# Attention and gated FFN in one kernel: a lead-in with 64x64 state products, one multiplication moved to GpSimd, and later scores for some pairs

## The chip, the cores and the metric

The kernel runs on one core of one Trainium2 chip. The metric is the device time of one execution in microseconds, the median of several runs. TensorE does the matrix products (PE in the profile), VectorE is DVE, ScalarE is ACT, GpSimd is POOL and SyncE is SP. DMAs are asked for by an instruction on SP, ACT or POOL and move data on 16 DMA engines.

## The reference, cut to what matters

Two layers run one after the other. The first is linear attention with decay, for 4 batches, 8 heads, 768 tokens and head size 64, in blocks of 64 tokens with a state of 64x64 for each head:

```python
for b in range(nb):
    intra = einsum('bhic,bhjc->bhij', qb, kb) * Dmask      # scores, masked
    intra = einsum('bhij,bhjd->bhid', intra, vb)           # values
    inter = einsum('bhid,bhde->bhie', qb * lam_pow, kv_state)
    out[:, :, sl] = intra + inter
    kv_state = lam_block * kv_state + einsum('bhsd,bhse->bhde', kb_dec, vb)
```

The second is a feed-forward layer on the 3072x512 result: `h = x @ w_in` (512x2048), `g = h * cos(h)`, and the output `g @ w_out` (2048x512).

## The kernel before, in words

**Tiles.** The tokens are cut into 24 blocks of 128. Two blocks, one from each of two batches, make a pair. The feed-forward layer takes the blocks in tiles of 4, 2, 2, 2, 2, 2, 2, 4 and 4. For each tile it makes 16 hidden blocks (`hidden`, L729 to L734: four matmuls each, with 128 columns of `w_in` as weights and the tile's tokens moving), turns each into `g` by a cosine on ACT (L738) and a product on DVE (L744), and multiplies by `w_out` (`project`, L774 to L779).

**The lead-in.** The first four blocks are two spans of 256 tokens, built in `add_span` (L579 to L687). A span is loaded as one DMA for q and one for k (SP, 512 KB each) and one for v (POOL). q and k are multiplied by powers of the decay (`prep`, L592), in two halves of four heads (hp 0 and 1); they are turned on PE (L601) and copied out by ACT (L604). Then come the scores (L612), their mask on DVE (L617, four for each span), the state product of k and v (`update`, L620 to L626), its copy into a block-diagonal tile (`update_out`, L629), the values (L638), the part that the state carries over (L644), and the copy of the result into `xT` (L652). `QK`, `OUTS`, `VALUES_OUT` and `STATE_OUT` (L32 to L35) say which engine does which of these for span 0 and span 1. In the kernel before DVE does all of span 0's `prep` and span 1's q, and POOL does span 1's k.

**The first tile's hidden blocks.** Blocks f = 0 to 4 of tile 0 are made in two halves of 256 columns, `a` for the tokens of span 0 and `b` for those of span 1. Blocks 3a and 4a are ordered behind span 1's last product (L849). `w_in` comes in six pieces of 2, 2, 1, 3, 4 and 4 blocks (`W_IN`, L38), asked for on POOL with a conversion to bf16: piece 1 holds f = 0 and 1, piece 2 f = 2 and 3, piece 3 f = 4, piece 4 f = 5 to 7, piece 5 f = 8 to 11, piece 6 f = 12 to 15. Then come three pieces of `w_out`. Before, the third piece's request waits for span 1's k on POOL:

```python
            if x:
                w_t["in", 2].issue.deps.append(kt[hp])
```

**What sets the order.** A planner (`Planner`, L57 to L141) lays out all tasks ahead of time with costs, due times, PSUM banks and buffers; each engine then runs its tasks in the order of the planned starts. `SETUP` holds the time at which each engine is taken to be free, and each task's second argument its cost. So a changed cost changes the order of instructions and nothing else. From pair 3 on, q and k are turned by DMA (`transposes_dma`, L364); the planner takes their result as ready 1.2 us after the DMA's planned end (`T[pr, i].lat`, L372). Pairs 3 to 6 (`ALONE`) have scores and state products as a group of their own; later pairs have theirs inside the stretch of the pair before (`add_scores`, L394, and `add_stretch`, L458).

**Fill.** Until the first hidden block of 512 columns (f = 5), `keep_awake` (L861 to L871) puts matmuls without use into PE's planned gaps, in fp32 from a zeroed tile `blank`, or one of 512 columns in bf16 from the identity where the gap is 0.25 to 0.6 us.

Of the kernel before, what the change touches and what calls it, by code (L numbers as in the profile page):

```python
# [10 lines left out]
F32 = mybir.dt.float32  # L11
BF16 = mybir.dt.bfloat16
# [12 lines left out]
ATT = 0.95  # L25
LOAD_US = 1.22
ALONE = [3, 4, 5, 6]

APART = [3, 4, 5, 11]


QK = [{"q": ("DVE", "DVE"), "k": ("DVE", "DVE")}, {"q": ("DVE", "DVE"), "k": ("POOL", "POOL")}]  # L32
OUTS = [{"qT": ("ACT", "ACT"), "kT": ("ACT", "ACT")}, {"qT": ("ACT", "ACT"), "kT": ("ACT", "ACT")}]
VALUES_OUT = [("ACT", "ACT"), ("DVE", "ACT")]
STATE_OUT = [("ACT", "ACT"), ("ACT", "ACT")]  # L35
ORDER = "q0 k0 q1 k1 v0 v1 i0 i1 i2 i3 i4 i5 o0 o1 o2 q4 q5 k4 k5 o3"

W_IN = [2, 2, 1, 3, 4, 4]  # L38
# [18 lines left out]
class Planner:  # L57
# [1 line left out]

    LAT = {"PE": 0.2, "ACT": 0.06, "DVE": 0.08, "POOL": 0.1, "SP": 0.0, "DMA": 0.0, "SETUP": 0.0}  # L60

    SETUP = {"POOL": 3.7, "DVE": 4.4, "ACT": 6.0, "SP": 0.85, "DMA": 1.95}

    def __init__(self, bufs):
        self.tasks, self.bufs = [], bufs
# [79 lines left out]
def kernel(  # L145
# [10 lines left out]
    nc = tc.nc  # L156
    B, H, S, D = q.shape
    P = 128
# [19 lines left out]
    consts = ctx.enter_context(tc.tile_pool(name="consts", bufs=1))  # L178
# [16 lines left out]
    ident = consts.tile([P, P], BF16)  # L195
# [15 lines left out]
                                base=0, pattern=[[1, D]], channel_multiplier=-1)  # L211
    halfpi = consts.tile([P, 1], F32)
    nc.vector.memset(halfpi, math.pi / 2.0)
    blank = consts.tile([P, 4 * P], F32)
    nc.vector.memset(blank, 0.0)  # L215
    kv_bd = consts.tile([P, 2, NP, P], BF16)
    nc.vector.memset(kv_bd, 0.0)

# [8 lines left out]
    pl = Planner({**BUFS, "q_f": BUFS["ld"], "k_f": BUFS["ld"], "v_f": BUFS["ld"]})  # L227
# [3 lines left out]
    halves = [slice(i * D, (i + 1) * D) for i in range(2)]  # L231
# [60 lines left out]
    w_t, pace = {}, []  # L292
# [15 lines left out]
    T, So, Vo, d_t, Uo, Uo_sp = ({} for _ in range(6))  # L308
# [6 lines left out]
    def prepare(pr):  # L315

        b, c = where(2 * pr)
        early = 2 * pr < TILES[0] + 2
        vec = {"DVE": nc.vector, "POOL": nc.gpsimd}
        us = {"DVE": 0.69, "POOL": 1.05}  # L320
        pa = lambda part: prio_attn(2 * pr, part)

        def new_qk():
            if ("qk", pr) not in live:
                live["qk", pr] = toks.tile([P, 2, H, 2, D], BF16, tag="qk", bufs=BUFS["qk"], name="qk")
            return live["qk", pr]

        def prep_q(_, s, e):
            vec[e].tensor_mul(new_qk()[:, 0, :, s], live.pop(("q_f", 2 * pr + s)),  # L329
                              q_scale[:, c, :].unsqueeze(2).to_broadcast([P, H, D]))  # L330

        def prep_k(_, s):
            (nc.scalar.copy if early else nc.gpsimd.tensor_copy)(new_qk()[:, 1, :, s], live.pop(("k_f", 2 * pr + s)))  # L333

        def prep_v(_, s, e):
            live["v_s", 2 * pr + s] = toks.tile([P, H, D], BF16, tag="v_s", bufs=BUFS["v_s"], name="v_s")
            vec[e].tensor_mul(live["v_s", 2 * pr + s], live.pop(("v_f", 2 * pr + s)),  # L337
                              v_scale[:, c, :].unsqueeze(2).to_broadcast([P, H, D]))

        a, k_ = [], []  # L340
        for s in range(2):
            n = 2 * pr + s
            eq = "DVE" if early and s == 0 else "POOL"
            ev = "DVE" if early and s == 1 else "POOL"
            a.append(pl.add(eq, us[eq], [load_t["q_f", n]] + a, partial(prep_q, s=s, e=eq), pa(-0.9), get=None if s else "qk"))
            k_.append(pl.add("ACT" if early else "POOL", 0.61, [load_t["k_f", n]] + ([] if early else [a[0]]), partial(prep_k, s=s), pa(-0.9)))
            d_t[n] = v_head[n] = pl.add(ev, us[ev], [load_t["v_f", n]], partial(prep_v, s=s, e=ev), pa(-0.85), get="v_s")
            for name, t in (("q_f", a[s]), ("k_f", k_[s]), ("v_f", d_t[n])):
                issue_t[name, n].frees = [t]

        def new_T():
            if ("qkT", pr) not in live:
                live["qkT", pr] = toks.tile([P, 2, H, P], BF16, tag="qkT", bufs=BUFS["qkT"], name="qkT")
            return live["qkT", pr]

        def transposes(t, i):
            live["t", pr, i] = bank(t.bank[0], [P, H, P], BF16, "ps_t")
            for h in range(H):
                nc.tensor.transpose(live["t", pr, i][:, h, :], live["qk", pr][:, i, h], ident)  # L359

        def transposes_out(_, i):
            nc.vector.tensor_copy(new_T()[:, i], live["t", pr, i])

        def transposes_dma(_, i):  # L364
            return nc.sync.dma_start_transpose(out=new_T()[:, i], in_=live["qk", pr][:, i].rearrange("t h s d -> t (h s d)"))

        for i, src in enumerate((a, k_)):
            get = None if i else "qkT"
            if 2 * pr >= DMA_FROM:
                head, T[pr, i] = dma("SP", 1.4, 1.3, partial(transposes_dma, i=i), 2 * pr + i - LAG + 1.5,  # L370
                                     src + ([qkT_head[pr]] if i else []), get=get, ordered=False)
                T[pr, i].lat = 1.2  # L372
                if i and 2 * pr + LAG < NBLK:
                    issue_t["q_f", 2 * pr + LAG].deps.append(head)
            else:
                t = pl.add("PE", MM(P, 8), src + ([T[pr, 0]] if i else []), partial(transposes, i=i), pa(-0.05 + 0.05 * i), banks=1)
                head = T[pr, i] = pl.add("DVE", 0.7, [t], partial(transposes_out, i=i), pa(0.0), get=get)
                t.bank_frees = [[head]]
            if i == 0:
                qkT_head[pr] = head  # L380
        qk_head[pr] = a[0]
# [194 lines left out]
    spans, span_deps = [], []  # L576
    span_v = [consts.tile([P, H, 2, D], BF16, name=f"v_sp{x}") for x in range(SPANS)]

    def add_span(x):  # L579
        pa = lambda part: -1000.0 + 2 * x + part  # L580
        pv = lambda part: -990.0 + 2 * x + part
        cut = [slice(4 * hp, 4 * hp + 4) for hp in range(2)]
        us = {"DVE": 0.69, "POOL": 1.04}
        vec = {"DVE": nc.vector, "POOL": nc.gpsimd}
        L = {name: consts.tile([P, 2, H, D], BF16, name=f"{name}_sp{x}") for name in ("q", "k")}
        L["v"] = span_v[x].rearrange("u h s d -> u s h d")
# [33 lines left out]
        def update(t):  # L620
            L["kv"] = bank(t.bank[0], [P, NP, P], F32, "ps_kv")
            rows = chunks[0][0]
            for p in range(NP):
                for s in range(2):
                    nc.tensor.matmul(L["kv"][:, p, :], lhsT=L["k"][rows, s, 2 * p:2 * p + 2, :], rhs=L["v"][rows, s, 2 * p:2 * p + 2, :],  # L625
                                     start=(p == 0 and s == 0), stop=True, skip_group_check=True)  # L626

        def update_out(_, h, e):
            (nc.scalar.copy if e == "ACT" else nc.vector.tensor_copy)(kv_bd[h, x, :, h], L["kv"][h, :, h])  # L629
# [27 lines left out]
        for hp in range(2):  # L657
# [1 line left out]
            a = pl.add(eq, us[eq], [load_t["q_f", "sp", x]], partial(prep, name="q", hp=hp, e=eq), pa(-0.9 + 0.1 * hp))  # L659
            kt.append(pl.add(ek, us[ek], [load_t["k_f", "sp", x]], partial(prep, name="k", hp=hp, e=ek), pa(-0.9 + 0.1 * hp)))  # L660
            if x:
                w_t["in", 2].issue.deps.append(kt[hp])
            outs = []
            for name, src in (("qT", a), ("kT", kt[hp])):
                e = OUTS[x][name][hp]
                t = pl.add("PE", MM(P, 4), [src, s_first if name == "kT" else None], partial(transposes, name=name, hp=hp), pa(-0.5 + 0.1 * hp), banks=1)
                outs.append(pl.add(e, 0.58 if e == "ACT" else 0.42, [t], partial(transposes_out, name=name, hp=hp, e=e), pa(-0.5 + 0.1 * hp)))
                t.bank_frees = [[outs[-1]]]
            s1 = pl.add("PE", 0.42, outs, partial(scores, hp=hp), pa(0.1 + 0.1 * hp), banks=2)
            if x and hp == 0:  # L670
                s_first = s1
            so[hp] = [pl.add("DVE", 0.69, [s1], partial(scores_out, hp=hp, i=i), pa(0.1 + 0.1 * hp + 0.05 * i)) for i in range(2)]
            s1.bank_frees = [[t] for t in so[hp]]

        u = pl.add("PE", 0.42, v_t + kt + [spans[0].get("carried")], update, pv(0.1), banks=1)
        Uo_sp[x] = [pl.add(e, 0.4 if e == "ACT" else 0.42, [u], partial(update_out, h=h, e=e), pv(0.1))
                    for h, e in zip(halves, STATE_OUT[x])]
        u.bank_frees = [Uo_sp[x]]
        span_deps.extend(v_t + kt)
        v0 = pl.add("PE", 0.35, so[0] + v_t + [spans[0].get("carried")], partial(values, hp=0), pv(0.2), banks=2)  # L680
        v1 = pl.add("PE", 0.35, [v0] + so[1], partial(values, hp=1), pv(0.25))
        second = pl.add("PE", MM(P, 4) + 0.1, [v1] + Uo_sp[x], carried, pv(0.3))
        for c, (t, e) in enumerate(zip((v1, second), VALUES_OUT[x])):
            Vo[2 * x + c] = [pl.add(e, 0.6 if e == "ACT" else 0.69, [t], partial(values_out, c=c, e=e), pv(0.3) if c == 0 else -1200.0)]
# [156 lines left out]
    pr = SPANS  # L841
# [16 lines left out]
    tc.plan = plan  # L858
    idle_ps = bank(idle.bank[0], [P, 4 * P], F32, "ps_idle")

    def keep_awake(us, at):  # L861

        cols = int((us - 0.06) * (1200.0 if at < 7.0 else 2400.0) / 4) // 64 * 64
        if us < 0.6:
            if us > 0.25:
                nc.tensor.matmul(idle_ps, lhsT=ident, rhs=ident.unsqueeze(1).to_broadcast([P, 4, P]), start=True, stop=True)
            return
        while cols > 0:
            n = min(cols, 4 * P)
            nc.tensor.matmul(idle_ps[:, :n], lhsT=blank[:, :P], rhs=blank[:, :n], start=True, stop=True)  # L870
            cols -= n  # L871

    keep_awake(1.2, 1.6)
    lam_ps = bank((idle.bank[0] + 4) % BANKS, [P, H], F32, "ps_lam")
    nc.tensor.matmul(lam_ps, lhsT=ones, rhs=lam_row, start=True, stop=True)
    lnl = consts.tile([P, H], F32)
# [14 lines left out]
    nc.scalar.activation(v_scale, expo, AF.Exp, scale=-1.0)  # L891
    warm = consts.tile([P, 1], F32)
    nc.scalar.activation(warm, halfpi, AF.Sin)
    now = 2.8
    for t in plan:
        if t.eng == "PE" and t.start < lead_end.start + 1e-6:
            keep_awake((t.start - now) * 0.95 if now < 3.0 else t.start - now, now)
            now = t.end
        if t.emit:
            t.ins = t.emit(t)  # L900

# [29 lines left out]
```

## Time and profile before

| What | Value |
|---|---|
| time, median of 3 runs | 202.96 us (202.85 to 203.05) |
| the profiled execution: its own time | 202.54 us |
| the profiled execution: its span, first to last instruction | 200.8 us |
| PE, PEld (weight load), DVE, ACT, POOL busy | 195.9, 116.8, 116.3, 119.4, 64.9 us |
| granted TensorE clock | 0.998 |
| HBM read and written | 27.26 and 6.29 MB |

All positions below are microseconds from the first instruction of the profiled execution. A line of the timeline gives the start, the length from the first start to the last end, the engine and the source line, what is written and read, and how many instructions are merged. Matmuls overlap in their records, so the start of the next group tells more than the end of the one before. A view of a tile gives, for each DMA request that it catches, the time from the request to the landing of the data.

### The profile page before, as it was taken

The numbers are of one execution on the slowest core, as the hardware profiler recorded it, in microseconds if no ns is written. First come the engines' busy times: TensorE is split into PE (matmuls) and PEld (weight loads), VectorE is DVE, ScalarE is ACT, GpSimd is POOL, SyncE is SP. The second block draws the span as 40 slices with busy tenths as digits, with TensorE's granted clock in tenths as the row PEclk, the third lists the DMA queues.
The fourth block names the chain that finished last, engine by engine and source line by source line (L and its number), as shares of the span: only waits on it lengthen the run. The fifth ranks groups of instructions, "written<-read, shape, count | busy, mean of one in ns | idle before, by whom it ended". The sixth has DMA issues, their size and how long they took to land.

```text
span 200.8 us, 5951 instructions
## 1 busy us (share of the span) xinstructions
PE 195.9 (98%) x2473; PEld 116.8 (58%) x2473; DVE 116.3 (58%) x230; ACT 119.4 (59%) x241; POOL 64.9 (32%) x85
## 2 busy tenths in 40 slices
PE   6999999999999999999999999999999999999994
PEld 3477444558757757766658676755445544444452
DVE  3978771269756948758458575835588354444001
ACT  4878771149658768666639666644887564345120
POOL 5893003085235360635555353545500000000000
PEclk9999999999999999999999999999999999999999
DMA  5999999999889997999999899979910010111112
GB/s 163 303 190 204 203 199 216 209 238 225 200 197 225 262 202 177 239 179 253 189 275 245 188 207 194 277 141 261 243 23 3 3 52 0 52 55 52 52 52 104
DMA packets 96620, 33.93 MB, mean 169 GB/s; under 512 B 84690, under 2 KB 93650, under 8 KB 96594
## 3 DMA queue, kind: packets, MB, share of 16 engines
q1 hardware_dynamic: 89088, 28.78, 63.2%
q0 software_dynamic: 7360, 4.72, 16.4%
q8 instruction: 19, 0.31, 0.7%
q10 hardware_dynamic: 146, 0.07, 0.1%
q14 instruction: 7, 0.06, 0.1%
HBM read 27.26 MB, written 6.29 MB: 167 GB/s over the span
## 4 chain that ended last, share of the span: by engine, by line
PE 95%; DMA 2%; ACT 0%; DVE 0%; SPq 0%; issue 0%; ACTq 0%; DVEq 0%
PE ps_h L732 42%; PE ps_f L778 42%; DMA sp_f<-in_k_dram 2%; PE ps_s L407 2%; PE ps_o L502 2%; PE ps_o L470 2%; PE ps_kv L419 1%; PE ps_t L601 1%; PE ps_s L612 1%; PE ps_o L638 1%; PE ps_kv L625 1%; PE ps_x L470 0%; PE ps_idle L870 0%; PE ps_t L359 0%; DVE k_sp L593 0%; PE ps_o L644 0%
## 5 line engine op out<-in xcount | busy, mean ns | idle before, releaser
L744 DVE TENSOR_TENSOR g<-ps_h,cos 128x256 bf16<-128x256 f32 (+1 forms) x149 | 73.1, 501 | 42.0 <-ACT cos L738 41.1
L738 ACT ACTIVATE cos<-ps_h,halfpi 128x256 f32<-128x256 f32 (+1 forms) x149 | 75.9, 536 | 29.3 <-PE ps_h L732 28.2
L778 PE MATMUL ps_f<-w_out_sb,g 128*128 128x512 bf16 (+2 forms) x400 | 91.4, 371 | 0.0
L732 PE MATMUL ps_h<-xT,w_in_sb 128*128 128x256 bf16 (+1 forms) x596 | 91.1, 303 | 0.0
L732 PEld LDWEIGHTS <-w_in_sb 128*128 128x128 bf16 x596 | 57.5, 98 | 30.1 <-DVE xT L510 0.4
L778 PEld LDWEIGHTS <-g 128*128 128x128 bf16 x400 | 37.6, 98 | 37.2
L329 POOL TENSOR_TENSOR qk<-q_f,q_scale 128x512 bf16<-128x512 f32 x19 | 20.0, 1067 | 34.7 <-DMA q_f<-in_q_dram 17.6
L792 ACT COPY o_sb<-ps_f 128x512 f32<-128x512 f32 (+1 forms) x24 | 13.7, 572 | 24.7 <-PE ps_f L778 24.5
L337 POOL TENSOR_TENSOR v_s<-v_f,v_scale 128x512 bf16<-128x512 f32 x19 | 19.6, 1042 | 9.8 <-DMA v_f<-in_v_dram 5.2
L412 DVE TENSOR_TENSOR s_m<-ps_s,mask 128x512 bf16<-128x512 f32 x20 | 13.0, 685 | 4.2 <-PE ps_s L407 3.6
L333 POOL CAST qk<-k_f 128x512 bf16<-128x512 f32 x18 | 11.0, 611 | 10.4 <-DMA k_f<-in_k_dram 10.2
L510 ACT CAST xT<-ps_o 128x512 bf16<-128x512 f32 x11 | 6.0, 588 | 9.0 <-PE ps_o L502 5.6
L425 DVE TENSOR_TENSOR sum<-sum,ps_kv 128x512 f32<-128x512 f32 x15 | 10.2, 682 | 0.6
L430 ACT CAST S<-sum 128x512 bf16<-128x512 f32 x15 | 9.1, 616 | 0.9 <-DVE sum L425 0.8
L253 POOL DMA_DIRECT2D w_out_sb<-in_moe_w_out_dram x4 | 3.0, 784 | 15.8 <-DMA q_f<-in_q_dram 15.8
L792 DVE COPY o_sb<-ps_f 128x384 f32<-128x384 f32 x1 | 0.6, 557 | 11.6 <-DMA out_dram<-o_sb 11.6
L470 PEld LDWEIGHTS <-v_s 64*64 64x64 bf16 x320 | 4.0, 107 | 4.2 <-issue 3.4
L870 PE MATMUL ps_idle<-blank 128*128 128x512 f32 (+2 forms) x8 | 4.7, 707 | 1.7 <-DVE blank L215 1.7
L487 DVE COPY spare<-ps_o 1x1 f32<-1x1 f32 x6 | 0.9, 156 | 8.4 <-PE ps_o L470 8.4
L617 DVE TENSOR_TENSOR s_m_sp<-ps_s,mask_sp 128x512 bf16<-128x512 f32 x8 | 5.1, 684 | 1.2 <-PE ps_s L612 1.2
L470 PE MATMUL ps_o<-s_m,v_s 64*64 64x64 bf16 x256 | 5.2, 196 | 0.0
L502 PE MATMUL ps_o<-qkT,S 64*64 64x64 bf16 x304 | 4.9, 195 | 0.0
(76 smaller groups left out, 90.1 us busy)
## 6 DMA issues: line engine op xcount, KB each, us to landing
q_f<-in_q_dram SPq DMA_DIRECT2D x20, 256.0 KB, 3.9
k_f<-in_k_dram SPq DMA_DIRECT2D x20, 256.0 KB, 4.2
v_f<-in_v_dram SPq DMA_DIRECT2D x20, 256.0 KB, 5.1
out_dram<-o_sb SPq DMA_DIRECT2D x19, 256.0 KB, 2.5
w_out_sb<-in_moe_w_out_dram POOLq DMA_DIRECT2D x4, 512.0 KB, 12.4
sp_f<-in_q_dram SPq DMA_DIRECT2D x2, 512.0 KB, 4.9
sp_f<-in_k_dram SPq DMA_DIRECT2D x2, 512.0 KB, 5.5
w_in_sb<-in_moe_w_in_dram POOLq DMA_DIRECT2D x2, 512.0 KB, 8.9
```

The source lines that it names most:

```text
L329: vec[e].tensor_mul(new_qk()[:, 0, :, s], live.pop(("q_f", 2 * pr + s)), q_scale[:, c, :].unsqueeze(2).to_broadcast([P, H, D]))
L333: (nc.scalar.copy if early else nc.gpsimd.tensor_copy)(new_qk()[:, 1, :, s], live.pop(("k_f", 2 * pr + s)))
L337: vec[e].tensor_mul(live["v_s", 2 * pr + s], live.pop(("v_f", 2 * pr + s)), v_scale[:, c, :].unsqueeze(2).to_broadcast([P, H, D]))
L412: nc.vector.tensor_mul(t, live["s", pr][s], mask.unsqueeze(1).to_broadcast([P, H, D]))
L425: nc.vector.tensor_add(new, live["sum", pr, 0] if half else live["sum", pr - 1, 1], live["kv", pr][half])
L430: nc.scalar.copy(new_S(pr, half), live["sum", pr, half])
L470: yield lambda h=h: nc.tensor.matmul(o[halves[h % 2], h // 2], lhsT=live["v_s", n0 + s][m, h, :], rhs=live["s_m", n0 + s][m, h, :], start= ...
L732: nc.tensor.matmul(t[:, :n], lhsT=w_in_sb[:, kd, f * P:(f + 1) * P], rhs=live["xT", i][:, kd, at], start=(kd == 0), stop=(kd == KD - 1))
L738: nc.scalar.activation(c[:, :n], live["h", i, f, at.start][:, :n], AF.Sin, bias=halfpi)
L744: return nc.vector.tensor_mul(live["g", i][:, f, at], live.pop(("h", i, f, at.start))[:, :n], live.pop(("c", i, f, at.start))[:, :n])
L778: nc.tensor.matmul(live["f", i, j, piece][:, :width], lhsT=live["g", i][:, f, j * P:(j + 1) * P], rhs=w_out_sb[:, f, part], start=(f == 0) ...
L792: (nc.scalar.copy if eng == "ACT" else nc.vector.tensor_copy)(o[:, :width], live["f", i, j, piece][:, :width])
```

## The change

The state products of a span become 16 matmuls of 64x64 instead of 8 of 64x128. Span 1's second q half goes from DVE to POOL, the second half of span 0's state copy and the second of its two copies into `xT` go from ACT to DVE. The request for piece 2 of `w_in` (and so all requests behind it on POOL) goes behind span 1's k, instead of that for piece 3. The transposes of pairs 4 to 9 are planned as ready later. Some planned costs are altered. The tile `blank` and its memset go; the fill reads a constant of one that the program's start sets, in fp32 and in bf16, with other lengths, and a fill is put behind the products with the decay.

```diff
+T_LAT = {4: 3.0, 5: 3.0, 6: 3.0, 7: 2.5, 8: 2.5, 9: 2.5}
-QK = [{"q": ("DVE", "DVE"), "k": ("DVE", "DVE")}, {"q": ("DVE", "DVE"), "k": ("POOL", "POOL")}]
+QK = [{"q": ("DVE", "DVE"), "k": ("DVE", "DVE")}, {"q": ("DVE", "POOL"), "k": ("POOL", "POOL")}]
-VALUES_OUT = [("ACT", "ACT"), ("DVE", "ACT")]
-STATE_OUT = [("ACT", "ACT"), ("ACT", "ACT")]
+VALUES_OUT = [("ACT", "DVE"), ("DVE", "ACT")]
+STATE_OUT = [("ACT", "DVE"), ("ACT", "ACT")]
-    SETUP = {"POOL": 3.7, "DVE": 4.4, "ACT": 6.0, "SP": 0.85, "DMA": 1.95}
+    SETUP = {"POOL": 3.7, "DVE": 4.2, "ACT": 6.1, "SP": 0.85, "DMA": 1.95}
-    blank = consts.tile([P, 4 * P], F32)
-    nc.vector.memset(blank, 0.0)
-                T[pr, i].lat = 1.2
+                T[pr, i].lat = T_LAT.get(pr, 1.2)
-        us = {"DVE": 0.69, "POOL": 1.04}
+        us = {"DVE": 0.62, "POOL": 1.02}
                 for s in range(2):
-                    nc.tensor.matmul(L["kv"][:, p, :], lhsT=L["k"][rows, s, 2 * p:2 * p + 2, :], rhs=L["v"][rows, s, 2 * p:2 * p + 2, :],
-                                     start=(p == 0 and s == 0), stop=True, skip_group_check=True)
+                    for i, h in enumerate(halves):
+                        nc.tensor.matmul(L["kv"][h, p, h], lhsT=L["k"][rows, s, 2 * p + i, :], rhs=L["v"][rows, s, 2 * p + i, :],
+                                         start=(p == 0 and s == 0), stop=True, skip_group_check=True)
             if x:
-                w_t["in", 2].issue.deps.append(kt[hp])
+                w_t["in", 1].issue.deps.append(kt[hp])
-            s1 = pl.add("PE", 0.42, outs, partial(scores, hp=hp), pa(0.1 + 0.1 * hp), banks=2)
+            s1 = pl.add("PE", 0.33, outs, partial(scores, hp=hp), pa(0.1 + 0.1 * hp), banks=2)
-        u = pl.add("PE", 0.42, v_t + kt + [spans[0].get("carried")], update, pv(0.1), banks=1)
+        u = pl.add("PE", 0.28, v_t + kt + [spans[0].get("carried")], update, pv(0.1), banks=1)
...
-    keep_awake(1.2, 1.6)
+    def ones_of(n, dt=BF16):
+        one = nc.const_aps.tensor(1.0, [P, 4 * P], dt)
+        nc.tensor.matmul(idle_ps[:, :n], lhsT=one[:, :P], rhs=one[:, :n], start=True, stop=True)
+
+    def keep_awake(us, slow):
+        if slow:
+            cols = min(int((us - 0.04) * 1200.0) // 64 * 64, 4 * P)
+            if cols > 0:
+                ones_of(cols)
+        elif us > 0.8:
+            ones_of(min(int((us - 0.25) * 600.0) // 64 * 64, 4 * P), F32)
+        elif us > 0.5:
+            ones_of(4 * P)
+
+    ones_of(4 * P, F32)
...
+    ones_of(4 * P, F32)
+    now = None
     for t in plan:
         if t.eng == "PE" and t.start < lead_end.start + 1e-6:
+            slow = t.start < 8.5
+            if now:
+                keep_awake(t.start - now, slow)
+            now = max(t.end, t.start + 0.4) if slow else t.end
```

The planned costs of the masks (0.69 to 0.61) and of the values (0.35 to 0.33) are altered in the same way.

More of the change, by code (lines that the diff above doesn't have):

```diff
@@ L668, in add_span @@
                 t.bank_frees = [[outs[-1]]]
-            s1 = pl.add("PE", 0.42, outs, partial(scores, hp=hp), pa(0.1 + 0.1 * hp), banks=2)
+            s1 = pl.add("PE", 0.33, outs, partial(scores, hp=hp), pa(0.1 + 0.1 * hp), banks=2)
             if x and hp == 0:
                 s_first = s1
-            so[hp] = [pl.add("DVE", 0.69, [s1], partial(scores_out, hp=hp, i=i), pa(0.1 + 0.1 * hp + 0.05 * i)) for i in range(2)]
+            so[hp] = [pl.add("DVE", 0.61, [s1], partial(scores_out, hp=hp, i=i), pa(0.1 + 0.1 * hp + 0.05 * i)) for i in range(2)]
             s1.bank_frees = [[t] for t in so[hp]]
-        u = pl.add("PE", 0.42, v_t + kt + [spans[0].get("carried")], update, pv(0.1), banks=1)
+        u = pl.add("PE", 0.28, v_t + kt + [spans[0].get("carried")], update, pv(0.1), banks=1)
         Uo_sp[x] = [pl.add(e, 0.4 if e == "ACT" else 0.42, [u], partial(update_out, h=h, e=e), pv(0.1))
@@ L679, in add_span @@
         span_deps.extend(v_t + kt)
-        v0 = pl.add("PE", 0.35, so[0] + v_t + [spans[0].get("carried")], partial(values, hp=0), pv(0.2), banks=2)
-        v1 = pl.add("PE", 0.35, [v0] + so[1], partial(values, hp=1), pv(0.25))
+        v0 = pl.add("PE", 0.33, so[0] + v_t + [spans[0].get("carried")], partial(values, hp=0), pv(0.2), banks=2)
+        v1 = pl.add("PE", 0.33, [v0] + so[1], partial(values, hp=1), pv(0.25))
         second = pl.add("PE", MM(P, 4) + 0.1, [v1] + Uo_sp[x], carried, pv(0.3))
@@ L859 @@
     idle_ps = bank(idle.bank[0], [P, 4 * P], F32, "ps_idle")
[L861 to L871, printed above, removed]
-    keep_awake(1.2, 1.6)
+    def ones_of(n, dt=BF16):
[11 more added lines that the diff above has]
+    ones_of(4 * P, F32)
     lam_ps = bank((idle.bank[0] + 4) % BANKS, [P, H], F32, "ps_lam")
@@ L893 @@
     nc.scalar.activation(warm, halfpi, AF.Sin)
-    now = 2.8
+    ones_of(4 * P, F32)
+    now = None
     for t in plan:
         if t.eng == "PE" and t.start < lead_end.start + 1e-6:
-            keep_awake((t.start - now) * 0.95 if now < 3.0 else t.start - now, now)
-            now = t.end
+            slow = t.start < 8.5
+            if now:
+                keep_awake(t.start - now, slow)
+            now = max(t.end, t.start + 0.4) if slow else t.end
         if t.emit:
```

## The prediction, made before the changed kernel ran

> **What bounds the kernel now.** I first read the page's busy times and the list of PE's waits.
>
> ```profile
> PE 195.9 (98%) x2473; PEld 116.8 (58%) x2473; DVE 116.3 (58%) x230; ACT 119.4 (59%) x241; POOL 64.9 (32%) x85
> PE ps_idle L870 <- DVE blank L215: 1.7, 1, 1.7
> PE ps_t L601 <- DVE k_sp L593: 0.3, 1, 0.3
> ```
>
> PE waits twice, both before 7.1 us. The chain of waits agrees: from 7.08 to 197.9 it is PE alone, 95% of the span. Its long pieces run at one rate (64 hidden matmuls of 256 columns in 7.02 us, 0.110 us each; 28 of 512 in 6.04 us, 0.216 us each). So no wait is left to remove after the lead-in. Next I read PE's timeline of the lead-in.
>
> ```profile
> 9.23 0.40 PE L601 MATMUL ps_t<-ident,q_sp 128*128 128x128 bf16 x4
> 9.47 1.08 PE L870 MATMUL ps_idle<-blank 128*128 128x512 f32 x2
> 10.57 0.40 PE L601 MATMUL ps_t<-ident,k_sp 128*128 128x128 bf16 x4
> 10.90 0.62 PE L625 MATMUL ps_kv<-v_sp,k_sp 64*128 64x128 bf16 x8
> 11.45 0.42 PE L638 MATMUL ps_o<-s_m_sp,v_sp 64*64 64x128 bf16 x16
> 11.69 0.39 PE L612 MATMUL ps_s<-qT_sp,kT_sp 64*64 64x128 bf16 x16
> 12.02 0.40 PE L601 MATMUL ps_t<-ident,k_sp 128*128 128x128 bf16 x4
> 12.35 0.42 PE L638 MATMUL ps_o<-s_m_sp,v_sp 64*64 64x128 bf16 x16
> 12.70 0.40 PE L644 MATMUL ps_o<-qT_sp,kv_bd 128*128 128x128 bf16 x4
> 13.03 0.62 PE L625 MATMUL ps_kv<-v_sp,k_sp 64*128 64x128 bf16 x8
> 13.57 0.42 PE L612 MATMUL ps_s<-qT_sp,kT_sp 64*64 64x128 bf16 x16
> 13.82 0.39 PE L638 MATMUL ps_o<-s_m_sp,v_sp 64*64 64x128 bf16 x16
> 14.14 1.48 PE L732 MATMUL ps_h<-xT,w_in_sb 128*128 128x256 bf16 x12
> 15.56 0.42 PE L638 MATMUL ps_o<-s_m_sp,v_sp 64*64 64x128 bf16 x16
> 15.91 0.40 PE L644 MATMUL ps_o<-qT_sp,kv_bd 128*128 128x128 bf16 x4
> ```
>
> The useful stream starts at 10.57, when POOL has scaled the first half of span 1's k: it lands at 9.3 and POOL starts at 9.47 (1.04 us each half). From there PE never stands still for long. The question is whether PE's own work or something just beneath it sets that pace. The weight loads and the landings of w_in answer it.
>
> ```profile
> 16.69 2.29 PEld L732 LDWEIGHTS <-w_in_sb 128*128 128x128 bf16 x20 [0.23 <-DMA w_in_sb<-in_moe_w_in_dram]
> ...
> L253 POOL DMA_DIRECT2D w_in_sb<-in_moe_w_in_dram x1: 760/760/760, 12.3 to 12.3; - x1
> DMA to landing us min/median/max: 6.1/6.1/6.1
> ```
>
> The last two lines are piece 4's, from the view of that tile: asked for at 12.3, landed at 12.3 + 6.1 = 18.4. In the same way piece 1 lands at 7.0 + 6.5 = 13.5, piece 2 at 7.7 + 7.2 = 14.9, piece 3 at 11.5 + 5.2 = 16.7, piece 5 at 21.0, piece 6 at 23.5. Against that stand PE's first uses: block 0 at 14.14, block 2 (third of the group at 14.14, 0.44 us each) at 15.0, block 4a at 16.7, where the weight load does wait, and block 5, the first of 512 columns, at 18.45 (five half blocks lie between 16.14 and 18.45). **Slack: 0.6, 0.1, 0, and 0.1 us.** The lead-in runs level with the w_in queue. Later pieces have more: block 8 comes near 22, a microsecond behind its piece.
>
> **What the Trainium skill says.** "TensorE: Matmul & The Clock Gate", Part 3, says that small matmuls on separate row and column tiles overlap in the array. The trace agrees: 16 values matmuls of 64x64 with 128 columns take 0.24 us (11.45 to 11.69), 15 ns each, against 0.55/8 = 69 ns for one of 64x128. The same page, Part 1, says that the array runs at half clock until it has been busy for a window of about 3.4 us; here four transposes take 0.40 us at 5.62 as at 12.02, so the clock is full from 5.6 on. "GPSIMD Engine Reference", Specifications, says that POOL shares its SBUF interface with DVE instructions of two SBUF inputs; no row of before has the two at once. "DMA: Bandwidth & Descriptors", Specifications, gives about 1 us to the first byte for a request on POOL; the trace shows only requests to an already full queue.
>
> **The change, part by part.** The sum is against the profiled execution (202.54 us; span 200.8 and 1.74 around it), which lies 0.42 below the median.
>
> 1. *State products.* One takes 0.55 us (10.90 to 11.45). The new one has 16 matmuls in two column tiles over one row tile. Nearest rows: the span state L697, also two column tiles, 32 in 0.62 us of the chain, 19 ns each, so 0.31; and the values on four tiles, 0.24. I take 0.29: **0.26 saved each, 0.5 us for two**, all on PE's stream.
> 2. *q to POOL.* DVE loses 0.61 us (8.42 to 9.02), so span 0's four masks end at 11.1 instead of 11.5. POOL gains 1.04. It is free from 8.5 to 9.47 now, and without piece 2's request (0.77 us) from 7.77; span 1's q lands at 7.8. So it ends near 8.9 and k starts at 9.47 as before: 0. If the shared interface makes it wait for DVE's half (until 8.45), it ends at 9.5: 0.05 late. The queue behind it on POOL is k, then w_in.
> 3. *Two copies to DVE.* ACT loses 0.37 + 0.6, DVE gains about 0.42 + 0.69. DVE idles 0.63 before 12.13 and 0.61 before 14.03, and starts 0.4 earlier, so the last mask still ends near 15.3. Values of span 1 wait for it; they ran at 15.56. 0, at worst 0.2.
> 4. *Piece 2's request.* It goes from 7.74 to 11.5, and pieces 3 to 6 and w_out, queued on POOL behind it, each 0.75 us later. The queue still holds piece 1, landing at 13.5. With 0.8 us of issue and the page's 1 us (an estimate) piece 2's data can start at 13.3: it fits with 0.2 to spare. So landings stay: 0, up to 0.3 if POOL is late.
> 5. *Fill and constants.* 1.7 us of waiting for `blank` goes, but q and k landings (4.7, 6.2) set the start: 0. The fill's idle stretch, 9.47 to 10.55, is hidden by k.
> 6. *Scores further on.* Each later group still pays its own entry and exit, about 0.09 us each (values to transposes and back). PE has no wait for transposes, which land 1.7 to 4.4 us before their scores; none to gain. Nor do I see two groups meet. 0, between -0.2 (one meeting) and +0.2 (a hidden run that finds its xT late).
>
> The sum of PE's work is -0.5. **But it doesn't reach the end.** Blocks 0 and 2 can't start before 13.6 and 15.0, and block 5 not before 18.4: the freed time becomes waiting for w_in, and at block 5 only 18.45 - 18.4, about 0.05 us, is left. After that the stream is as before. 202.54 - 0.05 + 0.42 = 202.9; with 0.1 for the small delays of items 2 to 4, **203.0 us, no change**.
>
> **The rivals.** *Faster: the saved work counts in full.* If the planner puts the second halves of blocks 3 and 4 (0.44 each) before block 5, w_in has 0.9 us of slack, and the 0.5 us is gained: 202.96 - 0.55 = 202.4. For it: the planner orders by ready times, and shorter costs can tip it. Against it: in its costs too the lead-in's end hangs on w_in. w_out's third piece, landed at 31.1 and first used by the fourth group of projections near 31.6 (28.99 and three groups of 0.86), caps this at about 0.5.
>
> *Slower: piece 2 is late.* Piece 3 has half of piece 2's bytes, yet lands 1.7 us after it, where piece 2 takes 1.4 after piece 1. The DMA view of 14.2 to 15.4 shows one packet of the instruction queue (0.02 MB) there, and all 16 engines must deliver before a piece counts as landed. PE's instructions are fetched in such packets, and the change puts 8 more matmuls and their loads ahead of that point and has PE there sooner, so the packet can fall on piece 2 instead. Then piece 2 lands at up to 15.9, PE stands at block 2 for up to 0.9, and values, carried product and blocks 3a and 4a are queued behind. Block 5 comes 0.3 to 0.85 late: 203.6. It decides from a landing past 15.0. A late POOL (item 4) ends the same way. Against it: it needs both order and moment to fall so.
>
> **How the numbers follow.** No change 0.42 (own range 202.7 to 203.3), faster 0.26 (202.4), slower 0.32 (203.6). The ends: 202.3 is the full saving and 0.1 of meeting groups; 203.8 is the full 0.85. A clock that falls to half by the shorter fill could cost 1 us more; I leave it outside. About 0.2%, 0.4 us, is what a measurement of this kernel can tell from no change. The cases give faster 0.25, same 0.43, slower 0.32.
>
> **What would show it.** Right: state products of 0.25 to 0.31 us; POOL's k still at 9.47; PEld waiting for w_in inside 13.5 to 18.4; block 5 between 18.4 and 18.6; the stretches after it as long as before. Wrong: block 5 before 18.3 or a piece landed earlier (faster), block 2 after 15.3 (slower), PE waiting for transposes, xT or banks after 20 us, or transposes longer than 0.40 us after 10 us (clock).

## The result, and the profile after

**Slower by about 1%: 205.51 us** (204.63 to 208.06, 6 runs) against 202.91 (202.78 to 203.05, 6 runs) in the same session; the ratio is 1.0113, 95% interval 1.0091 to 1.0134. The forecast was no change, 203.0, and its range ended at 203.8. A later session gave 205.39 against 202.75, ratio 1.0131 (1.0118 to 1.0144).

The first profiled execution of the changed kernel was a slow one (208.06 us, with 3.4 us of TensorE at half clock), so the lines below are of a second profiled execution of the same kernel (205.24 us, span 203.5, clock 1.00). In its source the state product is L625, hidden blocks are L732, projections L778 and the fill L863. First the page's busy times and PE's list of waits:

```profile
PE 197.9 (97%) x2488; PEld 117.1 (58%) x2488; DVE 115.9 (57%) x230; ACT 118.0 (58%) x239; POOL 66.4 (33%) x86
PE ps_h L732 <- DMA w_in_sb<-in_moe_w_in_dram: 0.9, 2, 0.5
PE ps_f L778 <- DMA w_out_sb<-in_moe_w_out_dram: 0.5, 1, 0.5
```

Before, PE itself waited for no weights. Now it waits for w_in twice and for w_out once. The timeline of PE has the two places of w_in (in brackets the wait in front of a group and who ended it):

```profile
11.02 0.38 PE L625 MATMUL ps_kv<-v_sp,k_sp 64*64 64x64 bf16 x12
11.21 0.24 PE L638 MATMUL ps_o<-s_m_sp,v_sp 64*64 64x128 bf16 x2
11.23 0.23 PE L625 MATMUL ps_kv<-v_sp,k_sp 64*64 64x64 bf16 x4
11.29 0.83 PE L638 MATMUL ps_o<-s_m_sp,v_sp 64*64 64x128 bf16 x30
...
14.76 0.61 PE L732 MATMUL ps_h<-xT,w_in_sb 128*128 128x256 bf16 x4
15.80 0.61 PE L732 MATMUL ps_h<-xT,w_in_sb 128*128 128x256 bf16 x4 [0.42 <-DMA w_in_sb<-in_moe_w_in_dram]
...
19.99 1.26 PE L732 MATMUL ps_h<-xT,w_in_sb 128*128 128x512 bf16 x6 [0.52 <-DMA w_in_sb<-in_moe_w_in_dram]
```

Of the kernel before, the start of block 5, the first of 512 columns:

```profile
18.45 0.81 PE L732 MATMUL ps_h<-xT,w_in_sb 128*128 128x512 bf16 x3
```

The state product is done in 0.27 us (11.02 to 11.29, with two matmuls of the values in between), as forecast. But block 2 starts at 15.80 instead of 15.03, and block 5 at 19.99 instead of 18.45: **1.54 us late**. (A wait is shorter than the delay that it leaves, since the records of the matmuls before it end later than the next one could start.) POOL's own timeline shows that the request was not late by POOL's work:

```profile
7.94 1.44 POOL L592 TENSOR_TENSOR q_sp<-sp_f,q_sp 128x512 bf16<-128x512 f32 x1 [0.16 <-DMA sp_f<-in_q_dram]
9.41 2.04 POOL L592 TENSOR_TENSOR k_sp<-sp_f,k_sp 128x512 bf16<-128x512 f32 x2
11.40 0.81 POOL L252 DMA_DIRECT2D w_in_sb<-in_moe_w_in_dram  x1
```

The view of the tile `w_in_sb` for this request:

```profile
DMA to landing us min/median/max: 4.4/4.4/4.4
```

k starts at 9.41 (9.47 before) and piece 2 is asked for at 11.4, as the prediction had it. It lands 4.4 us later, at 15.75 instead of 14.94; pieces 3 to 6 follow at 17.50, 19.94, 23.50 and 26.03, that is 0.8, 1.6, 2.5 and 2.5 us late. The chain of waits now goes through these requests:

```profile
9.41 2.04 POOL k_sp L592 x2
11.46 3.72 POOL w_in_sb L252 x5
15.18 1.40 POOL w_out_sb L252 x2
16.58 17.09 DMA w_out_sb<-in_moe_w_out_dram
33.72 3.61 PE ps_f L778 x16
```

Before, the chain was PE alone from 7.08. Now POOL's k and its row of requests stand in it up to 33.7 us: w_out's third piece, behind all of w_in, is 2.6 us late as well (33.68 against 31.12), and PE's projections wait for it. From block 5 to there the delay grows from 1.54 to 2.3 us; the last projection ends 2.7 us later than before.

### The profile page after: what moved, and what is told of

Read it like the earlier page. It is cut to its first block, busy times and chain, and to the rows that moved or that the text cites. A ratio compares the mean times of both kernels' runs of the same rounds, so it can differ in the third digit from the quotient of the medians.

```text
span 206.3 us, 5953 instructions
## 1 busy us (share of the span) xinstructions
PE 196.0 (95%) x2460; PEld 117.7 (57%) x2488; DVE 115.9 (56%) x230; ACT 118.1 (57%) x239; POOL 66.4 (32%) x86
## 4 chain that ended last, share of the span: by engine, by line
PE 87%; DMA 6%; issue 2%; POOL 2%; ACT 1%; SPq 0%; ACTq 0%; POOLq 0%
PE ps_h L732 40%; PE ps_f L778 39%; DMA sp_f<-in_q_dram 3%; DMA w_in_sb<-in_moe_w_in_dram 3%; PE ps_o L501 2%; PE ps_s L406 2%; PE ps_o L469 1%; PE ps_kv L418 1%; POOL k_sp L592 1%; POOL q_sp L592 1%; ACT cos L738 1%; SPq L252 0%; PE ps_x L469 0%; ACT xT L509 0%; PE ps_t L358 0%
## 5 line engine op out<-in xcount | busy, mean ns | idle before, releaser
L732 PE MATMUL ps_h<-xT,w_in_sb 128*128 128x256 bf16 (+1 forms) x591 | 90.6, 307 | 2.5 <-DMA w_in_sb<-in_moe_w_in_dram 2.2
L778 PE MATMUL ps_f<-w_out_sb,g 128*128 128x512 bf16 (+2 forms) x377 | 86.3, 370 | 3.3 <-issue 1.7
L732 PEld LDWEIGHTS <-w_in_sb 128*128 128x128 bf16 x596 | 58.5, 99 | 31.2 <-DMA w_in_sb<-in_moe_w_in_dram 2.4
L778 PEld LDWEIGHTS <-g 128*128 128x128 bf16 x400 | 37.5, 98 | 39.6 <-issue 1.1
L520 DVE TENSOR_TENSOR xT<-ps_o,cross 128x256 bf16<-128x256 f32 x8 | 3.1, 422 | 5.2 <-PE ps_o L501 5.2
L863 PE MATMUL ps_idle<-const-float32-1.0 128*128 128x512 f32 (+1 forms) x6 | 5.1, 945 | 0.8 <-PEq L920 0.8
```

Source lines behind the costliest of these rows:

```text
L732: nc.tensor.matmul(t[:, :n], lhsT=w_in_sb[:, kd, f * P:(f + 1) * P], rhs=live["xT", i][:, kd, at], start=(kd == 0), stop=(kd == KD - 1))
L778: nc.tensor.matmul(live["f", i, j, piece][:, :width], lhsT=live["g", i][:, f, j * P:(j + 1) * P], rhs=w_out_sb[:, f, part], start=(f == 0) ...
```

## The experiments

All times are medians of one session beside the kernel before in that session; "a" kernels start from the kernel after, "b" kernels from before. f = 5 stands for the start of the first block of 512 columns in the profile (18.45 before).

**1. The planned readiness of the transposes, undone in after and done alone.**

```diff
-T_LAT = {4: 3.0, 5: 3.0, 6: 3.0, 7: 2.5, 8: 2.5, 9: 2.5}
+T_LAT = {}
```

> The changed kernel with the planned latency of the DMA transposes back at 1.2 us for all pairs; everything else changed. Theory 1 (the loss has two parts: piece 2 of w_in late because its request is late, and a wait of PE for ACT near 134 us that the later scores make): the second part goes, about 1.0 us, so 204.5 against 205.5, with PE's waits free of the cosine and block 2 still waiting for w_in. Theory 2 (all of the loss is the late piece, and the wait near 134 us only a sequel of it): 205.5 as the changed kernel.

Measured: 205.02 against 202.99, ratio 1.0092 (1.006 to 1.0124), halfway between the two theories.

The kernel before with after's T_LAT, and nothing else:

> The kernel before with only the planned latencies of pairs 4 to 9 changed. Theory 1: 203.9 (202.9 and 1.0), with a wait of PE for ACT between 125 and 140 us and nothing else changed before 60 us. Theory 2: 202.9 and no wait.

Measured: 203.05, ratio 1.0005 (0.9984 to 1.0025). The later scores alone cost nothing that this interval, 0.5 us either way, can tell. The first profile of the changed kernel had shown a wait of 1.0 us for a cosine on ACT at 137 us; neither this run nor the second profile of the changed kernel has it.

**2. The late request alone, and after without it.**

```diff
-                w_t["in", 2].issue.deps.append(kt[hp])
+                w_t["in", 1].issue.deps.append(kt[hp])
```

> The kernel before with only piece 2's request behind span 1's k (piece 3's is no longer tied to it). Theory 1: piece 2 lands after 16 us instead of 14.9, PE waits 1 to 2.5 us at block 2, 204.2 or more. Rival (piece 2 is late because PE's instruction packet falls on it, which needs the extra matmuls and the earlier PE): landing stays near 15.0 to 15.3 and the time at 203.0 to 203.2.

Measured: 205.58, ratio 1.01 (1.0057 to 1.0143); piece 2 lands at 16.25, f = 5 is at 20.10. **This one line alone gives a loss of that size.**

Then after with the request back at piece 3 (the same two lines the other way round):

> The changed kernel with piece 2's request back ahead of span 1's q and k on POOL, piece 3's behind k, as before; q stays on POOL, so it starts 0.77 us later. Theory 1: piece 2 lands at 15.0 to 15.3, the wait at block 2 goes; k is 0.3 to 0.6 late on POOL; the later scores' 1.0 us stays: 203.9 to 204.3. Rival (instruction packet): piece 2 still lands at 15.5 or later and PE waits there; 204.8 to 205.5.

Measured: 204.01, ratio 1.004 (1.002 to 1.0061); pieces land as before (15.26, 16.75, 18.44), PE waits for no w_in, f = 5 at 18.86. So 1.5 of the 2.6 us go when the request is put back. What is left, 0.8 us by the ratio and 1.0 by the medians, has another source.

**3. Why the late request is late.** The data of piece 2 could start at 13.3 by the prediction, with piece 1 moving until then. The first test put more bytes into piece 1.

```diff
-W_IN = [2, 2, 1, 3, 4, 4]
+W_IN = [3, 1, 1, 3, 4, 4]
```

(with the request of the second piece behind k)

> The kernel before with the request for piece 2 of w_in behind span 1's k, and with pieces of 3 and 1 blocks in place of 2 and 2 at the head of w_in: piece 1 brings 384 KB instead of 256, so that the transfer engines still have work when the data of the late request can start. Theory (the queue of the transfer engines runs dry between the end of piece 1 and the start of piece 2, near 13.0 us, and everything behind lands 2 us later): the rate has no hole near 13 us, piece 2 lands at 15 to 15.3, piece 3 at 16.7 to 17, piece 4 at 18.4 to 18.9, PE does not wait for w_in for more than 0.3 us in all, 203.0 to 203.5 us. Rival (a request made late lands some 4.5 to 5.9 us later whatever the queue holds, or the requests behind it are what is late): the landings stay as with the late request alone, piece 4 at 20 or later, PE waits for w_in for 0.5 us and more, 204.5 us and more.

Measured: 204.3 against 202.84, ratio 1.0072 (1.0056 to 1.0088). Neither number was hit. Block 5's piece lands at 19.91 and PE waits 1.2 us for it, which is near the rival: the hole did not close, it moved. The second test put the same 512 KB as before ahead of k, but in one request:

```diff
-W_IN = [2, 2, 1, 3, 4, 4]
+W_IN = [4, 1, 3, 4, 4]
```

(`ORDER` names one piece fewer; the second piece is block 4's, behind k as before)

> The kernel before with one request of 512 KB (four blocks) in place of w_in's first two of 256 KB, and the next piece (128 KB, block 4) behind span 1's k as before: again only one request stands ahead of k, but as many bytes as before. Theory (what counts is the bytes queued ahead of a late request: 256 KB gave a deficit of 2 us, 384 KB of 1.3): the rate has no hole before 17 us, block 4's piece lands near 16.7 and blocks 5 to 7's near 18.4, as before; only blocks 0 and 1 wait, until the 512 KB land at 14.6 to 15.0, so that the first block of 512 columns comes at 18.9 to 19.4; 203.2 to 203.8 us. Rival (a request made behind k is late whatever stands ahead of it): block 5's piece lands at 19.5 or later, 204.3 us and more.

Measured: 203.64 against 202.74, ratio 1.0049 (1.0037 to 1.0061); the pieces of block 4 and of blocks 5 to 7 land at 16.59 and 18.27, as before, and PE waits for neither. f = 5 is at 19.47 all the same, since blocks 0 and 1 must now wait for 512 KB and the planner puts a fill of 1.35 us ahead of them. The rates of the transfers in two stretches tell the four apart (the last number of a line is GB/s; the one ahead of it is the busy share of the 16 engines, above 1 where packets overlap). Before:

```profile
13.00:15.00 2.00, 2.00 (x50) 1.64 (x49) 1.39 (x3) 1.84 (x6) 2.00 (x4) 1.00 1.56 195
15.00:18.00 3.00, 3.00 (x42) 2.30 (x41) 2.65 (x7) 2.75 (x7) 1.72 (x3) 1.00 1.33 203
```

The late request alone, with 256 KB of w_in ahead of k:

```profile
13.00:15.00 2.00, 2.00 (x64) 1.57 (x53) 1.39 (x3) 1.99 (x5) 2.00 (x4) 1.00 1.15 139
15.00:18.00 3.00, 2.34 (x35) 1.52 (x34) 2.31 (x6) 1.85 (x5) 2.53 (x4) 1.00 1.10 116
```

With 384 KB ahead of k:

```profile
13.00:15.00 2.00, 2.00 (x50) 1.57 (x48) 1.39 (x3) 1.68 (x5) 2.00 (x4) 1.00 1.66 183
15.00:18.00 3.00, 3.00 (x44) 2.49 (x42) 2.52 (x6) 2.71 (x7) 2.51 (x4) 1.00 0.99 129
```

With 512 KB ahead of k, in one request:

```profile
13.00:15.00 2.00, 2.00 (x44) 1.41 (x43) 1.39 (x3) 1.61 (x5) 2.00 (x3) 1.00 1.43 199
15.00:18.00 3.00, 3.00 (x42) 2.42 (x41) 1.71 (x5) 1.86 (x5) 1.70 (x3) 1.00 1.33 204
```

Against before, 256 KB ahead of k leaves out (195 - 139) x 2 + (203 - 116) x 3 = 373 KB by 18 us, which at 200 GB/s is 1.9 us; 384 KB leaves out 246 KB, 1.2 us; 512 KB nothing. f = 5 came 1.65 us late in the first and 1.51 in the second. The busy share falls with the rate in the first (1.15 against 1.56), so fewer packets were under way at a time. In all three kernels one request stands ahead of k and the next is made at 11.5 us, so **the bytes queued ahead of the late request decide how many are missing afterwards**, not the mere fact that it is late. Two things limit this. The sizes of the requests behind k change along (256, 128 and 384 KB in the first, 128, 128 and 384 in the second, 128 and 384 in the third), and no run holds them fixed. And 512 KB ahead is no safe number. In the profiled execution of experiment 1's second kernel (204.35 us, well above that kernel's median), whose requests stand in the order of before, span 1's q and k landed 0.7 us later and the requests behind k began at 12.19. Pieces 1 and 2 were 0.7 us late too, so the queue ahead lasted as long, and still the rate fell:

```profile
15.00:18.00 3.00, 3.00 (x43) 2.45 (x42) 2.81 (x6) 2.64 (x7) 2.45 (x4) 1.00 1.12 133
```

f = 5 was at 19.94 there, 1.49 us late. So an order of requests like that of before can lose its rate too; what tips it is not shown.

A last try, with the request behind span 1's q:

```diff
-                w_t["in", 2].issue.deps.append(kt[hp])
+                w_t["in", 1].issue.deps.append(a)
```

> The kernel before with the request for piece 2 behind span 1's q instead of at once, which also puts pieces 2 and 3 ahead of k on POOL. Theory: the request comes at 8.5 to 9.8 us, 3 us ahead of the end of piece 1 at 13.0, so that the rate has no hole and landings are as before; k starts at about 10 us instead of 9.47 and costs 0.2 to 0.5: 202.9 to 203.4 us. Rival (any delay of the request costs): pieces 4 and 5 land 0.5 us later or more, 204 us and more.

Measured: 204.66, ratio 1.0091 (1.0076 to 1.0106), above what the theory gave. It tells little: such a dependency only orders the plan, so pieces 2 and 3 were asked for at 7.73 and 8.46, ahead of k, which started at 9.43. The transfers had no hole, but piece 4 landed at 18.42, as before, while the planner had ordered PE's work otherwise, with a fill of 1.66 us at 16.61, and block 5 came at 20.97. PE waits for no w_in in that profile, so the loss seems to come with the order; no run tests that.

**4. What else loses: one part at a time.**

```diff
-QK = [..., {"q": ("DVE", "DVE"), "k": ("POOL", "POOL")}]
+QK = [..., {"q": ("DVE", "POOL"), "k": ("POOL", "POOL")}]
```

> The kernel before with nothing changed but the second half of span 1's q, multiplied on POOL instead of DVE. Theory (what is left of the loss when the request is put back comes from this): POOL is still busy with its requests until 8.5 us, then takes 1.04 us for q (up to 1.45 beside DVE), so k starts at 9.8 to 9.95 instead of 9.47, the transposes of k and all behind them come 0.3 to 0.45 us later; 203.3 to 203.6 us. Rival (the lead-in's end hangs on the landings of w_in, so that a late k costs nothing): 202.8 to 203.1 us with k late all the same.

Measured: 202.87 against 202.84, ratio 1.0004 (0.9994 to 1.0015); k at 9.60, f = 5 at 18.61. Then the smaller state products alone:

```diff
-                    nc.tensor.matmul(L["kv"][:, p, :], lhsT=L["k"][rows, s, 2 * p:2 * p + 2, :], ...)
+                    for i, h in enumerate(halves):
+                        nc.tensor.matmul(L["kv"][h, p, h], lhsT=L["k"][rows, s, 2 * p + i, :], ...)
```

(the operands are cut here; the planned cost goes from 0.42 to 0.28 us)

> The kernel before with nothing changed but the state products of the two spans, as 16 matmuls of 64x64 instead of 8 of 64x128 (planned cost 0.28 instead of 0.42). Theory of the prediction (each state product saves 0.26 us of PE's time, but the first tile's blocks wait for w_in instead): 202.8 to 203.0 us, the first block of 512 columns still at 18.4. Rival (the time saved counts in full): 202.3 to 202.5 us, that block at 18.0. A second rival (the changed tile shape costs the saving at the entry and exit of each group): 203.0 us, with no new wait for w_in.

Measured: 203.56, ratio 1.0035 (1.0022 to 1.0048). **Slower by 0.7 us**, which no theory had; f = 5 is at 19.24. The timeline of PE in that kernel (the line numbers are one higher here, so a hidden block is L733):

```profile
14.10 1.04 PE L733 MATMUL ps_h<-xT,w_in_sb 128*128 128x256 bf16 x8
15.06 0.46 PE L639 MATMUL ps_o<-s_m_sp,v_sp 64*64 64x128 bf16 x16
15.46 0.40 PE L645 MATMUL ps_o<-qT_sp,kv_bd 128*128 128x128 bf16 x4
15.69 0.27 PE L733 MATMUL ps_h<-xT,w_in_sb 128*128 128x256 bf16 x1
16.73 0.49 PE L733 MATMUL ps_h<-xT,w_in_sb 128*128 128x256 bf16 x3 [0.77 <-issue]
```

PE does one matmul of a block of four and stands until 16.73. Nothing holds it that the profile shows: the four belong together and wait for nothing between them. "issue" is the profile's word for that. Ahead of the standstill lies one packet of the instruction queue, in the DMA view of 14.3 to 14.4 us (packets, MB, share of 16 engines):

```profile
q8 instruction: 1, 0.02, 59.3%
```

59.3% of 16 engines over 0.1 us is 0.95 us on one engine. The packet started at 14.34, so it ended at 15.29, and PE went on 1.44 us after that. The smaller products put 16 more weight loads and 16 more matmuls of the two spans ahead of this place; before, by this count, PE came to it near 17.7. That PE stood for the packet is so far read from the order in time alone.

**5. Is it the number of instructions?** Matmuls without use, 16 and 32 pairs of weight load and matmul, ahead of the first fill, where PE idles:

```diff
+    one = nc.const_aps.tensor(1.0, [P, D], BF16)
+    for n in range(16):
+        nc.tensor.matmul(idle_ps[halves[n % 2], :D], lhsT=one[:D], rhs=one[:D], start=True, stop=True)
     keep_awake(1.2, 1.6)
```

> The kernel before with 16 matmuls of 64x64 without use, on a constant of one, put ahead of its first fill, where PE has nothing to do; nothing else is changed. Theory (PE stands still inside a hidden block because its next packet of 16 KB of instructions, which travels on the same transfer engines as w_in, starts near 14.3 us and can be used near 16.7; the smaller state products put 32 more weight loads and matmuls of both spans ahead of that point): 16 more pairs move that point forward by 32 records, from 17.7 to 16.2 us; PE stands there for about 0.5 us, with no semaphore, and the time is 203.2 to 203.4 us. Rival (the loss of the smaller state products is their own, from their shape or from the order): 202.8 to 203.0 us, no stall.

Measured: 204.02 against 202.75, ratio 1.0066 (1.005 to 1.0082).

> The same with 32 such matmuls. Theory: the point moves forward by 64 records to 15.6 us; PE stands there for 1.1 us until 16.7, the first block of 512 columns comes near 19.5 and the time is 203.8 to 204.1 us. Rival: 202.8 to 203.1 us.

Measured: 204.72, ratio 1.0101 (1.0081 to 1.0121). Idle matmuls in idle time cost 1.3 and 2.0 us: the number of instructions counts, but not by the way that I expected, since PE did not stand at 16.2 or 15.6. With 16, the packet fell on piece 2 (it started at 14.63; the first line is from the DMA view of 14.6 to 14.7), which landed at 7.7 + 9.0 = 16.7 instead of 14.9:

```profile
q8 instruction: 1, 0.02, 60.1%
16.74 0.61 PE L732 MATMUL ps_h<-xT,w_in_sb 128*128 128x256 bf16 x4 [1.40 <-DMA w_in_sb<-in_moe_w_in_dram]
```

The packet records of this trace show it directly. Each piece is closed by 16 packets of 4 bytes; 15 of piece 2's had ended by 14.50, and the last ended at 15.60, just after the instruction packet (14.63 + 0.96 = 15.59).

With 32 it started at 12.68, and piece 1 landed at 14.79 instead of 13.52 (block 0 waited 0.62). A later packet left PE standing inside a block at 130 us:

```profile
130.12 0.49 PE L732 MATMUL ps_h<-xT,w_in_sb 128*128 128x256 bf16 x3
132.25 0.72 PE L732 MATMUL ps_h<-xT,w_in_sb 128*128 128x256 bf16 x5 [1.64 <-issue]
```

That packet ran from 129.94 to 130.89, and PE went on 1.36 us after it: nearly the same gap as in the kernel with the smaller products. Two standstills at nearly one distance from a packet speak for the packet as their cause, but no run moves a packet and nothing else.

**6. Is this second loss in the changed kernel?**

```diff
-T_LAT = {4: 3.0, 5: 3.0, 6: 3.0, 7: 2.5, 8: 2.5, 9: 2.5}
+T_LAT = {}
-QK = [..., {"q": ("DVE", "POOL"), "k": ("POOL", "POOL")}]
+QK = [..., {"q": ("DVE", "DVE"), "k": ("POOL", "POOL")}]
-                w_t["in", 1].issue.deps.append(kt[hp])
+                w_t["in", 2].issue.deps.append(kt[hp])
```

> The kernel after with three parts undone: the times at which the transposes of pairs 4 to 9 are planned as ready, the request for piece 2 of w_in (back to before), and the second half of span 1's q (back to DVE). The smaller state products, the two copies on DVE, the new fill and the altered costs stay. Theory (the request and q on POOL are the whole loss): 202.7 to 203.0 us. Rival (the altered order, the copies or the fill lose as well): 203.4 us and more.

Measured: 203.5 against 202.84, ratio 1.0038 (1.0018 to 1.0059). Then with the old state products and their cost of 0.42 as well (the diff of the smaller products in 4, backwards):

> The kernel after with four parts undone: the planned readiness of the transposes, the request for piece 2, the second half of span 1's q, and the smaller state products (back to 8 of 64x128). The two copies on DVE, the new fill and the altered costs stay. Theory (what the earlier run with three parts undone lost came from the fill and a cold PE, which put span 1's products 0.4 us later, and from the copy on DVE that PE waited 0.3 us for; the smaller products gave back a part): 203.2 to 203.8 us. Rival (that loss was the instruction packet, reached too early by the smaller products): 202.8 to 203.0 us.

Measured: 202.72 against 202.75, ratio 1.0008 (0.9996 to 1.002): the rival's number. **Copies on DVE, fill, constants and altered costs are together worth nothing**, and the edits of the two kernels differ by the smaller products alone: again 0.6 to 0.7 us. The profile of the first of them has only 0.2 us of "issue" in front of a hidden block, though, and otherwise a late start behind the fill and a 0.3 us wait for xT; how the products cost their 0.7 there is not shown.

The kernel before with the late request of 2 and the smaller products of 4 together:

> The kernel before with two parts of the change, the late request for piece 2 and the 64x64 state products. Theory (when the transfers run dry at 13.0 the instruction packet goes there, so that PE never stands for it, and the smaller products cost nothing): no standstill without a semaphore inside a hidden block, 204.8 to 205.6 us, as with the late request alone. Rival (the losses of the two add up, 2.7 and 0.7 us): 205.9 us and more.

Measured: 204.67 against 202.74, ratio 1.0098 (1.0071 to 1.0126). PE has no standstill of the kind inside the lead-in's blocks: the packet went at 13.08, where the transfers thin out. The two losses alone, 1.0% and 0.35%, would add up to 1.35%, just beyond this interval. The first of them has 0.4% either way of its own, so that they don't add up is likely and not shown.

The changed kernel again, with no edit:

> The kernel after once more, for a second profile of it. Theory (the loss is w_in landing late): PE waits for w_in for 1.5 to 2.2 us in all at blocks 2 and 5, and the 1.0 us wait for ACT's cosine at 137 us, which the first profile showed, is not there; 205.0 to 205.6 us. Rival (the later scores cost 1 us at ACT's cosine): that wait is there again.

Measured: 205.39, ratio 1.0131 (1.0118 to 1.0144). The packet starts at 13.02 there, and the wait for a cosine is gone. The waits for w_in are 0.9 us in all, less than expected; with the 0.5 us for w_out they come to 1.4.

## Why the prediction was wrong

- **The step that failed is item 4**, "it fits with 0.2 to spare. So landings stay: 0, up to 0.3 if POOL is late". POOL was on time. The start was nearly right too: with the late request alone the rate falls only at 13.0. What was wrong is that the start of one piece was taken for the whole test. Piece 1 was all that was left in the queue, 256 KB fewer than before, and the transfers ran at 116 to 139 GB/s instead of about 200 for 5 us. The term had 0 to 0.3; with the request alone it measured 2.0 us (by the ratio, 1.2 to 2.9), and 1.5 us where it alone was put back. The 1 us to the first byte, taken from "DMA: Bandwidth & Descriptors", Specifications, is a figure for the first byte, which no view here dates. The rate, which the sum needed, falls 1.5 us after the request and is back at 198 GB/s only from 19.0, 7.5 us after it. Why the data behind the first come so thin no run settles.
- **The price of w_out was left out.** Item 4 counted the requests behind piece 2 as 0.75 us later each, but followed none to its use. w_out's third piece had 0.5 us of slack by the prediction's own rival (0.3 by the timeline: the projections start at 28.82, and twelve matmuls of 0.216 us later it is 31.41) and came 2.6 late; that adds 0.7 us.
- **Item 1** was right in size (0.27 us for a product, forecast 0.29) and right that it doesn't reach the end. It missed the price of 32 more records on PE's queue: 0.7 us alone. With the late request that price is not seen on top (ratio 1.0098 for the two, 1.01 for the request alone), though the intervals are too wide to rule it out.
- **Item 2** held: q on POOL costs nothing (1.0004, 0.9994 to 1.0015). Its worst case was the right one: POOL did not wait for DVE's half, but took 1.44 us beside it against 1.04 alone in the kernel with only q moved. It ended at 9.38, against 8.9 or at worst 9.5 in the sum, so k was not late. The 0.61 us that DVE was to gain did not come: with only q moved, the masks began at 9.02 as before, since they waited for the scores. The contention that "GPSIMD Engine Reference", Specifications, names between POOL and a DVE instruction with two SBUF inputs fits this, 1.44 us against 1.04.
- **Items 3 and 5** held (1.0008 together, 0.9996 to 1.002). **Item 6** held alone (1.0005). In company its share, by the ratios 1.0131 and 1.0092, may be anything up to 0.8 us, and isn't settled, nor is the split of the 0.8 us that after keeps when only its request is put back.
- **The slower rival** had the place right (block 2, from a landing past 15.0) and named a late piece 2. Its price, 203.6, was too small: it let block 5 come 0.3 to 0.85 late, and left the queue behind out. That piece 2 landed at 15.75, so near its 15.9, is luck. Its main mechanism, the instruction packet falling on piece 2, is not what happened: in the changed kernel the packet goes at 13.0, and one packet of 16 KB can't account for the 373 KB that are missing with the late request alone. But it exists: the run with 16 idle matmuls is that case, with 1.3 us.

## What to carry to other kernels

Before moving a DMA request later, count the bytes still queued ahead of it and follow every request behind it on that queue to its first use; here 512 KB ahead was enough for requests made at 11.5 us, and 256 KB cost 2 us, while one execution with requests at 12.2 lost 1.5 us with 512 KB ahead. Instructions in idle time are not free either: TensorE's program travels on the same 16 engines as the weights (the instruction queue in the DMA views), and here 32 more instructions cost 0.7 us in one kernel and 1.3 in another, where a piece came 1.75 us late.

## What the hardware showed that I had not expected

- A packet of TensorE's instructions (16 KB) takes about 0.95 us of one transfer engine, and PE resumed 1.44 and 1.36 us after its end in the two standstills seen.
- A piece counts as landed only when its last engine is through: 15 of 16 closing packets by 14.50, the last at 15.60, landing at 16.69.
- 16 useless matmuls of 64x64 in idle time cost 1.3 us, 32 cost 2.0 us.
- One multiplication of 512 columns on POOL took 1.44 us where it overlapped a DVE multiplication of 0.69 us, and 1.04 where it did not.
